# Attention and a token-and-channel mixer on one core: when ScalarE splits the next q and k, and in which order two mixing groups take their chunks

## The chip, the cores and the metric

The kernel runs on one core of a Trainium2 chip. The metric is device microseconds of one execution, the median of several runs. A profile is one further execution with the hardware profiler on; its own time stands beside the runs, because the sum of a prediction is made against the profiled execution.

## The reference, cut to what matters

Eight batches (B), eight heads (H), 576 positions (S), 64 columns a head (D), so 512 channels. Attention sees only the last 128 positions:

```python
scores = (q @ k.T) / sqrt(64) - slope[h] * |i - j|
scores = where(0 <= i - j < 128, scores, -1e9)
attn = softmax(scores)
x = concat_heads(attn @ v)                     # per batch 576 x 512
theta = x @ w_theta
zr, zi = x * cos(theta), x * sin(theta)
y = w_tok_r @ zr + w_tok_i @ zi                # mixes the 576 tokens
u = x + y
out = u + max(u @ w_ch, 0)
```

All products need more precision than one half-width pass gives, so the kernel splits an operand into a high and a low part and multiplies three times (high by high, high by low, low by high).

## The kernel before, in words

Attention works on **pairs** of heads, four pairs a batch. For a pair, `split_pair` (L330) turns the raw q and k (`qr`, `kr`, loaded by `load_pair`, L235) into the parts `qh`, `ql`, `kh`, `kl`: `qh` (L336) and `kh` (L339) are made by ScalarE (ACT), `ql` (L337) by VectorE (DVE), `kl` (L340) by GpSimd (POOL) behind `ql`. `qr` and `kr` are single buffers, so the next pair's load starts once these four have read them. `Pair.scores` multiplies the parts on TensorE (PE); `weigh` adds the bias and finds the row minimum on DVE (L427), and ACT takes the exponential (L430) in place. In the next slot `Pair.flip` turns four 128x128 blocks of the weights into a PSUM bank `t_ps` (L90); ACT copies the bank as the high half of `pt` (L442), DVE makes the low half (L443). There are two `t_ps` banks and four flips a pair. `Head.values` multiplies `pt` by the values (`acc`), and `finish` divides into `x_sb` (L478 to L481, DVE).

After the four pairs of a batch, `turn` goes over five blocks of tokens: it turns `x_sb` into columns (`x_hi`, `x_lo`), multiplies by `w_theta`, takes sine and cosine on ACT (L541 to L547), and writes the products as nine chunks of 128 rows, `z_hi` (ACT, L494 and L556) and `z_lo` (DVE or POOL, L495 and L557). Block 0 gives chunk 8, block 1 chunks 0 and 4, block 2 chunks 1 and 5, block 3 chunks 2 and 6, block 4 chunks 3 and 7.

`mix` (L589) multiplies the chunks by the token weights: eight groups g (half of the tokens by 128 channels), each with a PSUM bank of `ps_m` (three banks, shared with theta, `channels` and the first score tile) and nine chunks, three matmuls to a chunk, in the order 8, 0, 4, 1, 5, 2, 6, 3, 7. Each chunk is one step of a generator. `channels` multiplies the result by `w_ch` and adds it to the output.

**Order of work.** `attend` (L663) computes batch b's attention and at the same time takes steps of batch b-1's mixing. A slot is one pair: flips 0 and 2, `steps[0]` steps of mixing, the next pair's scores (tiles 0, 1, 2), `steps[1]` steps, flips 1 and 3, `steps[2]` steps, the first head's values, scores (tiles 3, 4), then `prepare(p + DEPTH + 2)`, which splits pair p+2 and loads pair p+3, `steps[3]` steps and the second head's values. From batch 2 on the steps of a batch's first slot are 7, 7, 6, 3; of batch 1's first slot 3, 11, 6, 3. I call the first slot of a batch, where the turn's chunks meet the mixing, the **join**.

PE's order is the order in which the code is traced (`keep_in_program_order`). The order on ACT, DVE and POOL is set by the scheduler at compile time, from its own estimates; `tc.issue_after(ins)` binds each instruction traced inside it to stand behind `ins`, but only those on the engine of `ins`. `prepare` stands inside `issue_after(done.ins)`, and `done` is on DVE (L481): `ql` is bound by it, `qh` and `kh` on ACT are not. Each engine works its queue in order, so an instruction that waits holds up all behind it.

Of the kernel before, what the change touches and what calls it, by code (L numbers as in the profile page):

```python
# [17 lines left out]
AF = mybir.ActivationFunctionType  # L18
# [8 lines left out]
PEXP = 14.0  # L27
# [3 lines left out]
DEPTH = 1  # L31
# [19 lines left out]
def attn_moe_kernel(ctx: ExitStack, tc: tile.TileContext, qt, kt, vx, wth, wtok, wch, band, out):  # L51
    nc = tc.nc
# [21 lines left out]
    def mm(*args, **kw):  # L74
        ins = nc.tensor.matmul(*args, **kw)  # L75
        if pinned:
            tc.keep_in_program_order(ins)

    def behind_all(some):
        stack = ExitStack()  # L80
        for ins in some:
            stack.enter_context(tc.issue_after(ins.ins))
        return stack
# [5 lines left out]
    def flipped(*args):  # L89
        ins = nc.tensor.transpose(*args)  # L90
        if pinned:
            tc.keep_in_program_order(ins)
# [142 lines left out]
    def load_pair(p):  # L235
        b, h = divmod(2 * p, H)
        q, kr = (qr_too, kr_too) if p == 1 else (qr, ld.tile([128, S], F32, name="kr"))
        nc.sync.dma_start(out=q[:64, :S], in_=qt[b, h])
        nc.sync.dma_start(out=q[64:, :512], in_=qt[b, h + 1, :, :512])
        nc.sync.dma_start(out=q[64:, S:], in_=qt[b, h + 1, :, 512:])  # L240
        nc.sync.dma_start(out=kr, in_=kt[b, h:h + 2].rearrange("h d s -> (h d) s"))
        return q, kr
# [39 lines left out]
    z_scale, copied = {}, []  # L282
# [95 lines left out]
    class Pair:  # L378
# [53 lines left out]
        def flip(self, bank):  # L432
            t_ps = ps_t.tile([128, 512], F32, name="t_ps")
            for n, (i, e, j) in enumerate(BANKS[bank]):
                flipped(t_ps[:, 128 * n:128 * n + 128], self.sc[i, e][:, 128 * j:128 * j + 128], ident)
            if self.early:
                pt = ptp.tile([128, 512], F32, name="pt")
                nc.scalar.copy(pt, t_ps)
                parts_of = [pt]
            else:  # L440
                pt = ptp.tile([128, 2, 512], F16, name="pt")
                copied.append(nc.scalar.activation(pt[:, 0], t_ps, AF.Copy, scale=2.0 ** PEXP))  # L442
                nc.vector.scalar_tensor_tensor(out=pt[:, 1], in0=t_ps, scalar=2.0 ** PEXP, in1=pt[:, 0],  # L443
                                               op0=ALU.mult, op1=ALU.subtract)
                parts_of = [pt[:, a] for a in range(2)]
            for n, (i, e, j) in enumerate(BANKS[bank]):
                for to in ((0, 1) if i == 0 else (e,)):
                    at = 128 * n + (64 * to if i == 0 else 0)
                    self.pt[i, to, j] = [t[:, at:at + 128] for t in parts_of]
# [139 lines left out]
    def mix(st):  # L589

        xtf, z_hi, z_lo = st["xtf"], st["z_hi"], st["z_lo"]
        u_hi = big.tile([128, 4, S], F32R, name="u_hi")
        u_lo = big.tile([128, 4, S], F32R, name="u_lo")
        st.update(u_hi=u_hi, u_lo=u_lo)
        banks = {}
        seq = (8, 0, 4, 1, 5, 2, 6, 3, 7)

        def part(g, ks):
            hf, m = divmod(g, 4)
            cs = slice(hf * HALF, hf * HALF + HALF)  # L600
            if g not in banks:
                banks[g] = ps_m.tile([128, 512], F32, name="mm")
            y_ps = banks[g]
            for k in ks:
                c = seq[k]
                for n, (z, w) in enumerate(((z_hi, wtk_hi), (z_hi, wtk_lo), (z_lo, wtk_hi))):
                    mm(y_ps[:, :HALF], z[:, c, m * 128:m * 128 + 128], w[:, c, cs],
                       start=(k == 0 and n == 0), stop=(k == 8 and n == 2))
                if k < 8:
                    yield  # L610
            if ks[-1] == 8:
                nc.vector.scalar_tensor_tensor(out=xtf[:, m, cs], in0=y_ps[:, :HALF], scalar=st["back"],  # L612
                                               in1=xtf[:, m, cs], op0=ALU.mult, op1=ALU.add)
                nc.scalar.copy(u_hi[:, m, cs], xtf[:, m, cs])  # L614
                def low(m=m, cs=cs):
                    return nc.gpsimd.tensor_tensor(out=u_lo[:, m, cs], in0=xtf[:, m, cs],  # L616
                                                   in1=u_hi[:, m, cs].bitcast(F32), op=ALU.subtract)

                if st["b"] + 1 < B:
                    lows.append(low)  # L620
                else:
                    low()
                yield

        begun = 2 if st["b"] + 1 < B else 3
        for ks in (range(7), range(7, 9)):
            for g in range(begun):
                yield from part(g, ks)
        for g in range(begun, 8):
            yield from part(g, range(9))  # L630
# [21 lines left out]
    def prepare(p):  # L652

        if 0 <= p - 1 < pairs and p - 1 not in parts:
            parts[p - 1] = split_pair(p - 1, raw.pop(p - 1))
        if p < pairs and p not in raw:
            raw[p] = load_pair(p)
# [5 lines left out]
    def attend(b, x_sb, mixing, chans, first, behind, lowered):  # L663

        for g in range(H // 2):
            p = b * H // 2 + g
            pair = first.pop(0)
            one, two = pair.heads
            new = None
            if p + DEPTH < pairs:  # L670
                new = Pair(p + DEPTH)
                first.append(new)
            measured = []
            if p % 2 and p + 3 < pairs:
                measured.append(((p + 1) // 2 + 1, slice(0, 2)))
            elif p % 2 == 0 and p + 2 < pairs:
                if p == H // 2:
                    measured.append((p // 2 + 1, slice(0, 2)))
                measured.append((p // 2 + 1, slice(2, 4)))
            scaled = p // 2 + 1 if p % 2 and p + 1 < pairs else None  # L680

            def scores(tiles):
                if new is not None:
                    with tc.issue_after(lowered.ins) if b == 1 and g == 0 else nullcontext():
                        new.scores(tiles, behind)

            steps = STEPS[min(g, 2)] if b > 1 else FIRST[g]
            with behind_all((behind, lowered)) if b == 1 and g == 0 else nullcontext():
                pair.flip(0)
                pair.flip(2)  # L690
            step(mixing, steps[0])
            scores(SCORES[0])
            scores(SCORES[1])
            if measured and not (b == 1 and g == 0):
                with tc.issue_after(new.weighed.ins):
                    for some in measured:
                        measure(*some)
            step(mixing, steps[1])
            pair.flip(1)
            pair.flip(3)  # L700
            step(mixing, steps[2])
            if scaled:
                with tc.high_priority(FINISH):
                    spread_first(scaled)
            one.values()
            with tc.high_priority(FINISH):
                done = one.finish(x_sb)
            scores(SCORES[2])
            if scaled:
                with tc.high_priority(FINISH):  # L710
                    spread_scales(scaled)
            with tc.issue_after(done.ins):
                if b == 1 and g == 0:
                    for some in measured:
                        measure(*some)
                if new is not None:
                    new.heads[0].ready()
                prepare(p + DEPTH + 2)
                if b == 1 and g == 0:
                    with behind_all(new.exps):  # L720
                        step(late)
            step(mixing, steps[3])
            if g >= 2 and (b > 1 or g == 3):
                step(chans)
            two.values()
            with tc.high_priority(FINISH):
                done = two.finish(x_sb)
            if new is not None:
                with tc.issue_after(done.ins):
                    done = new.heads[1].ready()  # L730
                    for low in lows:
                        after(low(), done)
                    if b == 1 and g < 3:
                        with behind_all(new.exps):
                            step(late)
            else:
                for low in lows:
                    low()
            lows.clear()
# [156 lines left out]
```

## Time and profile before

| | |
|---|---|
| median of 3 runs (lowest to highest) | 707.63 us (706.1 to 710.97) |
| the profiled execution, its own time | 709.53 us |
| its span, first to last instruction | 707.8 us |
| PE busy | 666.3 us, 94% |
| DVE, ACT, POOL busy | 76%, 71%, 20% |
| mean granted TensorE clock | 0.971 |

The 1.7 us between span and time lie around the span. A matmul record is longer than the distance to the next matmul, because matmuls overlap, so PE's share is not its use at peak. [...]

### The profile page before, as it was taken

Reading aid. Unit: us, or ns where it says so; the run is one execution under the profiler, and the core shown is the slowest. Engines: PE = TensorE matmul, PEld = TensorE weight load, DVE = VectorE, ACT = ScalarE, POOL = GpSimd, SP = SyncE. Lnnn points to the kernel's source line nnn. Section 1 sums busy time; section 2 is a strip of 40 time slices with the busy share of each in tenths; the row PEclk is TensorE's granted clock in tenths of the full one; section 3 lists DMA queues with packets and bytes.
Section 4 is the critical chain, followed back from the end, with each engine's and each line's share of the span. In section 5 each row is a group of like instructions: output and inputs, shape, how many; then the busy total and the mean of one; then the engine's idle time right before and its main releaser. Section 6 shows DMA issues by size and latency. Waiting matters only on the chain.

```text
span 707.8 us, 15986 instructions
## 1 busy us (share of the span) xinstructions
PE 666.3 (94%) x6202; PEld 574.2 (81%) x6202; DVE 540.1 (76%) x1521; ACT 503.0 (71%) x1011; POOL 143.3 (20%) x199
## 2 busy tenths in 40 slices
PE   3779889899999999999999999999999999999998
PEld 2668667789888988888888888789888988889787
DVE  5997698996888769875888768786889768865722
ACT  6998687877957597757966697666976687645810
POOL 3010001440223121221212211211212211310220
PEclk9965998999999999999999999999999999999999
DMA  9943101531023201222022300322021210100001
GB/s 287 309 158 101 39 1 37 159 89 61 26 73 84 91 26 32 84 81 68 26 73 68 105 28 10 106 81 69 26 72 46 82 35 9 36 11 34 26 16 53
DMA packets 32620, 49.86 MB, mean 70 GB/s; under 512 B 5664, under 2 KB 22048, under 8 KB 32544
## 3 DMA queue, kind: packets, MB, share of 16 engines
q1 hardware_dynamic: 32544, 48.84, 22.6%
q8 instruction: 49, 0.80, 0.5%
q14 instruction: 27, 0.22, 0.1%
HBM read 39.39 MB, written 9.44 MB: 69 GB/s over the span
## 4 chain that ended last, share of the span: by engine, by line
PE 42%; ACT 24%; DVE 23%; DMA 6%; issue 2%; SPq 2%; POOL 0%; ACTq 0%; DVEq 0%; POOLq 0%
PE mm L75 30%; PE acc L75 4%; DMA kr<-in_kt_dram 4%; PE t_ps L90 4%; DVE pt L443 4%; ACT s_sb L430 4%; PE s_ps L75 3%; ACT g L546 3%; ACT z_hi L494 2%; ACT g L545 2%; DMA qr<-in_qt_dram 2%; DVE ql L337 2%; DVE g L550 2%; DVE s_sb L427 2%; DVE z_lo L495 2%
## 5 line engine op out<-in xcount | busy, mean ns | idle before, releaser
L75 PE MATMUL mm<-wtk_hi,z_lo 128*128 128x288 f16 x576 | 165.9, 288 | 3.1 <-DVE z_lo L495 3.0
L75 PE MATMUL mm<-wtk_hi,z_hi 128*128 128x288 f16 x576 | 166.2, 289 | 0.6 <-ACT z_hi L494 0.5
L75 PE MATMUL mm<-wtk_lo,z_hi 128*128 128x288 f16 x576 | 165.8, 288 | 0.0
L430 ACT ACTIVATE s_sb<-s_sb,fixed 128x256 f32<-128x256 f32 (+1 forms) x256 | 103.9, 474 | 56.7 <-DVE fixed L427 56.6
L75 PEld LDWEIGHTS <-z_hi 128*128 128x128 f16 x1152 | 109.4, 99 | 31.1 <-ACT z_hi L494 1.5
L443 DVE SCALAR_TENSOR_TENSOR pt<-t_ps,pt 128x512 f16<-128x512 f32 x116 | 76.4, 684 | 35.9 <-ACT pt L442 35.1
L427 DVE CUSTOM_DVE_ANT_0 s_sb<-s_ps,bands 128x256 f32<-128x256 f32 (+1 forms) x256 | 85.5, 384 | 0.3 <-PE s_ps L75 0.3
L75 PEld LDWEIGHTS <-z_lo 128*128 128x128 f16 x576 | 56.6, 98 | 20.8 <-DVE z_lo L495 6.5
L90 PE MATMUL t_ps<-fixed,s_sb 128*128 128x128 f32 x448 | 66.4, 287 | 1.7 <-DVE pt L443 1.7
L616 POOL TENSOR_TENSOR u_lo<-xtf,u_hi 128x288 fp32r<-128x288 f32 x64 | 50.0, 799 | 84.9 <-DVE vl L363 47.6
L442 ACT ACTIVATE pt<-t_ps 128x512 f16<-128x512 f32 x116 | 63.3, 580 | 5.1 <-PE t_ps L90 5.1
L75 PE MATMUL acc<-vh,pt 128*128 128x65 f16 x1044 | 59.7, 194 | 6.4 <-DVE pt L443 4.6
L340 POOL TENSOR_TENSOR kl<-kr,kh 128x576 fp32r<-128x576 f32 x31 | 45.4, 1464 | 99.2 <-DVE ql L337 52.7
L75 PEld LDWEIGHTS <-pt 128*128 128x128 f16 x1566 | 55.2, 98 | 11.0 <-DVE pt L443 6.0
L90 PEld LDWEIGHTS t_ps<-fixed,s_sb 128*128 128x128 f32 x448 | 54.8, 150 | 4.7 <-PE t_ps L90 1.6
L614 ACT CAST u_hi<-xtf 128x288 fp32r<-128x288 f32 x64 | 27.2, 425 | 43.3 <-DVE xtf L612 43.3
L362 POOL MEMSET vh<- 128x5 f16 x58 | 7.0, 121 | 243.2 <-PE acc L75 240.5
L75 PE MATMUL acc<-vl,pt 128*128 128x64 f16 x522 | 55.4, 193 | 0.0
L75 PE MATMUL mm<-wth_hi,x_hi 128*128 128x512 f32 x160 | 47.4, 418 | 1.5 <-DVE x_hi L512 1.5
L75 PE MATMUL mm<-u_hi,wch_hi 128*128 128x288 f32 x256 | 47.2, 306 | 0.0
L612 DVE SCALAR_TENSOR_TENSOR xtf<-mm,fixed,xtf 128x288 f32<-128x288 f32 x64 | 32.0, 509 | 18.7 <-PE mm L75 18.6
L75 PE MATMUL s_ps<-kh,qh 64*128 64x256 f32 (+1 forms) x256 | 44.8, 347 | 0.1
(158 smaller groups left out, 1514.9 us busy)
## 6 DMA issues: line engine op xcount, KB each, us to landing
vb<-in_vx_dram SPq DMA_DIRECT2D x16, 650.0 KB, 5.1
out_dram<-xtf SPq DMA_DIRECT2D x64, 144.0 KB, 1.8
kr<-in_kt_dram SPq DMA_DIRECT2D x31, 288.0 KB, 3.3
qr<-in_qt_dram SPq DMA_DIRECT2D x31, 144.0 KB, 2.8
qr<-in_qt_dram SPq DMA_DIRECT2D x31, 128.0 KB, 2.8
xtf<-in_wch_dram SPq DMA_DIRECT2D x4, 512.0 KB, 4.7
z_hi<-in_wtok_dram SPq DMA_DIRECT2D x2, 576.0 KB, 6.3
z_lo<-in_wtok_dram SPq DMA_DIRECT2D x2, 576.0 KB, 6.3
```

The lines of the kernel that those rows point to most:

```text
L75: ins = nc.tensor.matmul(*args, **kw)
L90: ins = nc.tensor.transpose(*args)
L337: low = nc.vector.scalar_tensor_tensor(out=ql, in0=qr, scalar=sc, in1=qh.bitcast(F32), op0=ALU.mult, op1=ALU.subtract)
L340: rest = nc.gpsimd.tensor_tensor(out=kl, in0=kr, in1=kh.bitcast(F32), op=ALU.subtract)
L427: self.weighed = nc.vector.tensor_tensor_reduce(out=sb, in0=ps, in1=bias, scale=2.0 ** -(2 * self.p % H + 1), scalar=3.0e38, op0=ALU.add, ...
L430: self.exps.append(nc.scalar.activation(sb, sb, AF.Exp, bias=least, scale=-1.0))
L442: copied.append(nc.scalar.activation(pt[:, 0], t_ps, AF.Copy, scale=2.0 ** PEXP))
L443: nc.vector.scalar_tensor_tensor(out=pt[:, 1], in0=t_ps, scalar=2.0 ** PEXP, in1=pt[:, 0], op0=ALU.mult, op1=ALU.subtract)
L546: nc.scalar.activation(g[:n], g[:n], AF.Sin, bias=halfpi[:n], scale=-RAD)
L612: nc.vector.scalar_tensor_tensor(out=xtf[:, m, cs], in0=y_ps[:, :HALF], scalar=st["back"], in1=xtf[:, m, cs], op0=ALU.mult, op1=ALU.add)
L614: nc.scalar.copy(u_hi[:, m, cs], xtf[:, m, cs])
L616: return nc.gpsimd.tensor_tensor(out=u_lo[:, m, cs], in0=xtf[:, m, cs], in1=u_hi[:, m, cs].bitcast(F32), op=ALU.subtract)
```

## The change

Two edits. `Pair.flip` remembers its copy (ACT, L442) as `self.copied`, and `prepare` now also stands behind `pair.copied`, the copy of the slot's last flip (flip 3), which binds `qh` and `kh` on ACT. And the first groups of `mix` take their chunks as five, two, two by turns, where they took seven, two.

```diff
             if self.early:
-                nc.scalar.copy(pt, t_ps)
+                self.copied = nc.scalar.copy(pt, t_ps)
...
-                copied.append(nc.scalar.activation(pt[:, 0], t_ps, AF.Copy, scale=2.0 ** PEXP))
+                self.copied = nc.scalar.activation(pt[:, 0], t_ps, AF.Copy, scale=2.0 ** PEXP)
+                copied.append(self.copied)
...
         begun = 2 if st["b"] + 1 < B else 3
-        for ks in (range(7), range(7, 9)):
+        for ks in (range(5), range(5, 7), range(7, 9)):
             for g in range(begun):
                 yield from part(g, ks)
...
-                prepare(p + DEPTH + 2)
+                with tc.issue_after(pair.copied.ins):
+                    prepare(p + DEPTH + 2)
```

In the changed file the lines from L443 on are one higher, and those from L718 on two.

ACT before, the last slot of a batch from the end of the slot before it, to the start of the turn (`pt` are the copies of flips 0 and 2, then of 1 and 3; `last` and `s_sb` the exponentials; L511 the turn's first copy):

```order
L361 ACTIVATE vh<-vb,fixed 128x5x64
L336 ACTIVATE qh<-qr 128x640
L442 ACTIVATE pt<-t_ps 128x512 x2
L339 CAST kh<-kr 128x576
L430 ACTIVATE last_104<-last_104,fixed 128x192
...
L442 ACTIVATE pt<-t_ps 128x512 x2
L614 CAST u_hi<-xtf 128x288
...
L336 ACTIVATE qh<-qr 128x640
L361 ACTIVATE vh<-vb,fixed 128x5x64
L339 CAST kh<-kr 128x576
L511 CAST x_hi<-t_ps 128x4x64
```

The same stretch of ACT in the change:

```order
L361 ACTIVATE vh<-vb,fixed 128x5x64
L442 ACTIVATE pt<-t_ps 128x512 x2
L430 ACTIVATE last_104<-last_104,fixed 128x192
...
L442 ACTIVATE pt<-t_ps 128x512 x2
L615 CAST u_hi<-xtf 128x288
L336 ACTIVATE qh<-qr 128x640
L339 CAST kh<-kr 128x576
...
L361 ACTIVATE vh<-vb,fixed 128x5x64
L512 CAST x_hi<-t_ps 128x4x64
```

`qh` and `kh` stood ahead of, between or behind the slot's first copies, one slot ahead of their `ql`, and once ahead of the turn's first copy; now they stand behind the copies of flips 1 and 3, in the slot of their `ql`. The order on SP, which issues the loads, is unchanged.

PE before, at a join from batch 2 on (matmuls of chunks; `mm_3662` is group 0's bank, `mm_3714` group 1's, `mm_3684` the first score tile, `t_ps_3736` flip 1):

```order
L75 MATMUL mm_3662<-wtk_hi_121,z_hi_3373 128x288
...
L75 MATMUL mm_3662<-wtk_hi_121,z_lo_3374 128x288
L75 MATMUL mm_3684<-kh_3297,qh_3295 128x192
...
L75 MATMUL mm_3714<-wtk_hi_121,z_hi_3373 128x288
...
L75 MATMUL mm_3714<-wtk_hi_121,z_lo_3374 128x288
L90 MATMUL t_ps_3736<-fixed_103,s_sb512_3264 128x128 x4
```

PE in the change, the same stretch (`mm_3678` is group 1's bank, `mm_3685` the first score tile):

```order
L75 MATMUL mm_3662<-wtk_hi_121,z_lo_3374 128x288
...
L75 MATMUL mm_3678<-wtk_hi_121,z_hi_3373 128x288
...
L75 MATMUL mm_3678<-wtk_hi_121,z_lo_3374 128x288
L75 MATMUL mm_3685<-kh_3297,qh_3295 128x192
...
L75 MATMUL mm_3678<-wtk_hi_121,z_hi_3373 128x288
...
L75 MATMUL mm_3662<-wtk_hi_121,z_hi_3373 128x288
...
L75 MATMUL mm_3678<-wtk_hi_121,z_lo_3374 128x288
L90 MATMUL t_ps_3736<-fixed_103,s_sb512_3264 128x128 x4
```

Ahead of the scores stood seven chunks of group 0; now five of group 0 and two of group 1. Behind them stood seven of group 1; now three of group 1, then chunks 2 and 6 for each group. Chunks 3 and 7 come behind the flips in both.

DVE before, at the same join (`z_lo` from `g` and `f` of block 4 are chunks 3 and 7):

```order
L443 SCALAR_TENSOR_TENSOR pt<-t_ps,pt 128x512
L550 SCALAR_TENSOR_TENSOR g<-x_sb,fixed,g 128x512
L427 ISA last_105,fixed<-mm,bands 128x192
...
L495 TENSOR_TENSOR z_lo<-g,z_hi 128x512
L427 ISA s_sb_3692,fixed<-s_ps,bands 128x128
...
L260 TENSOR_REDUCE peak_108<-vb 128x2
L495 TENSOR_TENSOR z_lo<-f,z_hi 128x512
```

DVE in the change:

```order
L444 SCALAR_TENSOR_TENSOR pt<-t_ps,pt 128x512
L427 ISA last_105,fixed<-mm,bands 128x192
...
L551 SCALAR_TENSOR_TENSOR g<-x_sb,fixed,g 128x512
...
L260 TENSOR_REDUCE peak_108<-vb 128x2
L496 TENSOR_TENSOR z_lo<-g,z_hi 128x512
L496 TENSOR_TENSOR z_lo<-f,z_hi 128x512
```

The weighing of the scores moved ahead of chunk 3's `z_lo`; the same instructions stand ahead of chunk 7's.

## Rows read from the trace of the kernel before

**Rows 1.** Windows view: us, busy of each engine, clock, DMA, GB/s; a whole batch.
```profile
255.00:330.00 75.00, 73.13 (x750) 63.48 (x749) 60.22 (x179) 53.27 (x111) 17.37 (x24) 1.00 0.23 66
```

**Rows 2.** Waits of PE (us in total, times, longest), 160 to 640 us.
```profile
PE acc L75 <- DVE pt L443: 2.6, 6, 0.5
PE mm L75 <- DVE z_lo L495: 2.1, 5, 0.4
PE mm L75 <- DVE x_hi L512: 0.7, 1, 0.7
PE acc L75 <- ACT pt L442: 0.6, 1, 0.6
PE t_ps L90 <- DVE pt L443: 0.6, 1, 0.6
```

**Rows 3.** Waits of PE's weight loads, 160 to 640 us.
```profile
PEld L75 <- DVE z_lo L495: 3.6, 5, 0.7
PEld L75 <- DVE pt L443: 3.6, 7, 0.6
PEld mm L75 <- DVE x_hi L512: 1.4, 3, 0.9
...
PEld L75 <- ACT pt L442: 0.9, 2, 0.7
```

**Rows 4.** Waits of ACT, 97 to 708 us.
```profile
ACT s_sb L430 <- DVE fixed L427: 55.3, 26, 3.6
...
ACT qh L336 <- DMA qr<-in_qt_dram: 14.3, 19, 2.1
ACT kh L339 <- DMA kr<-in_kt_dram: 12.1, 16, 2.4
```

**Rows 5.** Timeline of ACT (start us, us, what, [idle before]), a batch's last slot.
```profile
306.74 0.74 ACT L336 ACTIVATE qh<-qr 128x640 fp32r<-128x640 f32 x1 [0.59 <-DMA qr<-in_qt_dram]
307.39 1.06 ACT L442 ACTIVATE pt<-t_ps 128x512 f16<-128x512 f32 x2
310.86 0.67 ACT L339 CAST kh<-kr 128x576 fp32r<-128x576 f32 x1 [2.41 <-DMA kr<-in_kt_dram]
...
313.18 1.05 ACT L442 ACTIVATE pt<-t_ps 128x512 f16<-128x512 f32 x2
...
317.51 1.71 ACT L430 ACTIVATE s_sb<-s_sb,fixed 128x256 f32<-128x256 f32 x4 [2.96 <-DVE fixed L427]
```

**Rows 6.** Timeline of DVE, the same slot.
```profile
313.78 1.29 DVE L443 SCALAR_TENSOR_TENSOR pt<-t_ps,pt 128x512 f16<-128x512 f32 x2 [1.96 <-ACT pt L442]
...
316.32 0.81 DVE L337 SCALAR_TENSOR_TENSOR ql<-qr,qh 128x640 fp32r<-128x640 f32 x1
```

**Rows 7.** Timeline of all engines at a join: chunk 6, chunk 7, chunk 3.
```profile
268.41 0.10 PEld L75 LDWEIGHTS <-z_lo 128*128 128x128 f16 x1 [0.73 <-DVE z_lo L495]
...
272.92 0.68 DVE L495 TENSOR_TENSOR z_lo<-f,z_hi 128x512 f16<-128x512 f32 x1
...
273.29 0.29 PE L75 MATMUL mm<-wtk_hi,z_hi 128*128 128x288 f16 x1
...
273.41 0.29 PE L75 MATMUL mm<-wtk_lo,z_hi 128*128 128x288 f16 x1
```

**Rows 8.** Waits of PE, 97 to 160 us.
```profile
PE acc L75 <- DVE pt L443: 1.9, 2, 1.0
```

**Rows 9.** Waits of PE's weight loads, 97 to 160 us.
```profile
PEld L75 <- DVE z_lo L495: 1.7, 3, 0.9
```

**Rows 10.** Windows: batch 1's join, then its first slots.
```profile
103.00:109.60 6.60, 5.57 (x23) 2.44 (x21) 6.47 (x19) 6.57 (x12) 0.00 (x0) 0.50 0.00 0
118.00:147.00 29.00, 27.03 (x318) 22.91 (x318) 28.83 (x96) 23.47 (x51) 12.25 (x15) 1.00 0.44 129
```

**Rows 11.** Waits of PE, 640 to 708 us.
```profile
PE mm L75 <- DVE z_lo L495: 0.5, 1, 0.5
```

**Rows 12.** Waits of PE's weight loads, 640 to 708 us.
```profile
PEld L75 <- DVE z_lo L495: 1.2, 2, 0.8
```

## The prediction, made before the changed kernel ran

> **What bounds the kernel now.** I read the windows first: in one whole batch PE is busy 73.1 of 75 us, DVE 60.2, ACT 53.3 [rows 1]. So PE sets the pace, and an edit is worth what it takes out of PE's waits; ACT and DVE time counts only where PE stands behind it. Next come the waits, of PE and of its weight loads side by side [rows 2, 3]. The first are too short, because a matmul record lasts 0.29 us though the next one starts 0.12 us later [rows 7], so that part of a stop is hidden under the last record; the second are too long, since loads run ahead. The truth lies between. From 160 to 640 us PE stops for the low half of pt (2.6 to 3.6 us), for its high half (0.6 to 0.9), for a flip's bank that DVE has not read out (0.6), for the turn's first columns (0.7 to 1.4) and for z_lo (2.1 to 3.6). Third, who is late: ACT waits 14.3 us for the loads of qr and 12.1 us for kr [rows 4], in its queue, with other work behind.
>
> **Moving q and k on ACT (batches 2 to 7).** Nothing is added: the casts still take 0.74 and 0.67 us [rows 5], in another place. In a batch's last slot qh waited 0.59 us for its load and ran ahead of the first pt copies, and kh stood 2.41 us ahead of the exponentials, so the second pt copies came at 313.18 [rows 5]. DVE sat idle 1.96 us for them and made the low halves from 313.78 [rows 6], and PE waited for these. Without casts and waits the first copies can come 0.59 + 0.74 = 1.3 us earlier, and the exponentials by at least the 2.41 + 0.67 = 3.1 us that kh held them, if DVE has weighed the scores by then. The stops that are some 0.6 us long cannot survive that. Where the casts now stand, behind the second copies, ACT was idle before the next four exponentials (2.96 us here, 55.3 us in all [rows 5, 4]), and the two casts take 1.41 us of it. Behind them in ACT's queue stand a cast of u_hi, the exponentials, and vh; DVE's ql waits for qh, but starts only at 316.32 [rows 6], some 2 us after qh would end (copies to 314.2, one u_hi, then qh). The load has landed: kr's late one ended ACT's wait at 310.86 [rows 5]. SP's order is the same, and loads still start behind ql and kl, so qr and kr have most of a slot to land instead of being asked for on landing.
>
> I take the stops for pt at the upper bound, 3.6 + 0.9 = **4.5 us**, because they are many and short, where the matmul's record hides most; the bank's stop at **0.6 us**. The turn's first column copy stood behind qh, vh and kh with their waits, and now stands behind vh alone: **1.2 us**, near the upper bound of 1.4, as two of the three stops appear in the weight loads only. Together 6.3 us; bounds 4.5 (PE's rows, all of them) to 6.5, and zero if DVE is late by itself.
>
> **Five, two, two.** At five joins PE reaches chunk 6 before its z_lo is written (0.73 us in the load's row, 0.4 in PE's [rows 7, 2]). In the new order chunks 2 and 6 come behind the scores, and this stop goes. But what is late next is chunk 7. Its z_lo starts on DVE at 272.92 and lasts 0.68, so it ends at 273.60 [rows 7], with no idle time before it in its row, and the same DVE instructions stand ahead of it as before, so it does not come earlier. PE began chunk 3 at 273.29 and reads chunk 7's z_lo as the sixth matmul, 5 x 0.12 later, at 273.9. Started 0.6 us earlier it would read at 273.3, and must wait for 273.6, while chunk 3's z_lo has also moved back on DVE behind the weighing. So of 0.6 us a join I credit only 0.15, over five joins **0.7 us**; bounds 0 and the 3.6 us of rows 3. Where no attention follows, in the last batch, three groups now take fifteen chunks before block 3 is needed, and the stop goes: 0.5 to 1.2 us [rows 11, 12], I take **0.9**.
>
> **Batch 1.** [...] Eleven steps behind the scores are 33 matmuls; at half clock 0.24 us each, 7.9 us, so with seven chunks ready PE is busy throughout and part of the stops goes. I take 1.2. In the slots behind, PE waits 1.9 us for pt [rows 8], but DVE is busy 28.8 of 29 us there [rows 10]: DVE is the bound, and an earlier copy on ACT gives little. I take 0.8 of the 1.9. Together **2.0 us**; bounds 0 and 1.7 + 1.9 = 3.6.
>
> **Sum.** 6.3 + 0.7 + 0.9 + 2.0 = 9.9 us. Against the profiled execution's own 709.53 (span 707.8 and 1.7 around it) that gives 699.6; the median of the runs, 707.63, lies 1.9 lower and would give 697.7. I take **698.5**, between them.
>
> **Rivals.**
> *DVE takes over.* The stops for pt are put down to DVE, which also weighs, splits and divides. For it: DVE is full in batch 1 [rows 10], and at the joins it has no gap. Against: in later slots it idles for ACT (1.96 us in rows 6). If only half of the 6.3 us goes, nothing at the five joins, and 0.9 + 1.0 elsewhere, the gain is 5.1 us: 703.5 by the same middle. Chance 0.25.
>
> *TensorE's clock comes back sooner at batch 1's join.* The granted clock stood at 0.50 for the whole stretch in which PE kept stopping [rows 10]. With the stops gone, the same 33 matmuls at full clock take 4.0 us instead of 7.9. ACT's and DVE's work allows about 2 us of that, and if at the five joins the weighing delays chunk 7 less than I think (another 2 us), the gain is 13.9 us: 694.7. Chance 0.13. [...]
>
> *The casts wait for loads in their new place: slower.* They now stand ahead of the four exponentials and of ql, so a load that lands behind the second pt copies holds ACT, then DVE's ql and the weighing behind it. It decides where a load lands later than ACT's idle time covers, 2.96 - 1.41 = 1.5 us behind the copies [rows 5]. For it: kr's wait of 2.41 shows that loads can be late. Against: each load now has most of a slot. If one slot in each of seven batches waits 2.4 us uncovered and the gain for pt goes too, it is 7 x 2.4 - (9.9 - 6.3) = 13 us slower, 722 by the same middle. Chance 0.05.
>
> That the change does nothing is excluded: the three queues are in another order.
>
> **Chances and range.** The forecast has 0.57, its own range 694 to 703. About 1% (7.1 us) is what a measurement here can tell from no change, so faster means under 700.5. Of the forecast three quarters lie there, of the clock rival all, of DVE's hardly any: 0.57 x 0.75 + 0.13 + 0.01 = 0.57. Slower 0.05, the rest, 0.38, within 1%. The range for 8 in 10 reaches from 691 (all upper bounds, 6.5 + 3.6 + 1.2 + 3.6, and the clock's 2, are 16.9 under the median) to 705, which takes in DVE's rival.
>
> **What would show it.** Right: no wait of qh or kh for a DMA in ACT's waits; the stops for pt, and for the turn's first columns, gone from PE's; at the joins no stop at the sixth chunk, and a new, shorter one at chunk 3's or 7's z_lo behind the flips. Wrong: PE's waits for pt as long as before with DVE busy ahead of them (then DVE was the cause); joins shorter by 0.5 us each (then chunk 7 was not the limit); batch 1's 118 to 147 us much shorter (then ACT held DVE there); waits of qh for its load behind the second copies.

## The result and the profile after

| | before | changed |
|---|---|---|
| median of 13 runs each (lowest to highest) | 709.67 us (705.76 to 712.51) | 702.25 us (699.19 to 705.42) |
| ratio, 95% interval | | 0.9897 [0.9871, 0.9923] |
| profiled execution, own time and span | 709.53, 707.8 us | 699.19, 697.4 us |

The change is faster by 1.0%, 7.4 us by the medians (5.5 to 9.2 by the interval) and 10.3 us between the two profiled executions. The forecast was 698.5 us, its sum 699.6 for the profiled execution.

To see where the time went I cut every trace at the same four matmuls: the first transpose of each turn, the first scores and the first values of batch 1. For the changed kernel these rows of PE's timeline are the cuts (start us, us, what):

```profile
99.63 0.36 PE L75 MATMUL mm<-kh,qh 128*128 128x192 f32 x1 [1.50 <-DVE f L543]
...
113.49 0.19 PE L75 MATMUL acc<-vh,pt 128*128 128x65 f16 x1
...
161.41 0.38 PE L90 MATMUL t_ps<-fixed,x_sb 128*128 128x128 f32 x2
...
631.49 0.38 PE L90 MATMUL t_ps<-fixed,x_sb 128*128 128x128 f32 x2
```

The table has the distances between the cuts, from the traces of all kernels of this study ("join" is from the first scores of batch 1 to its first values, "slots" from there to batch 1's turn, "six batches" from there to the last turn, "end" the rest):

| kernel | start to batch 0's turn | turn to scores | join | slots | six batches | end |
|---|---|---|---|---|---|---|
| before | 76.32 | 24.99 | 12.77 | 47.08 | 479.76 | 66.83 |
| changed | 75.56 | 24.07 | 13.87 | 47.92 | 470.08 | 65.93 |
| changed, a second profile | 80.69 | 23.51 | 12.19 | 49.03 | 470.03 | 65.91 |
| casts alone | 75.22 | 25.85 | 12.88 | 47.89 | 471.20 | 66.83 |
| five, two, two alone | 81.07 | 25.08 | 12.20 | 47.06 | 480.42 | 65.91 |
| two load buffers | 81.72 | 24.89 | 14.48 | 46.68 | 471.21 | 66.82 |
| old place, two buffers | 82.34 | 22.73 | 13.05 | 47.75 | 478.16 | 66.82 |
| old place but for first slots | 82.48 | 25.72 | 14.72 | 47.78 | 471.28 | 66.82 |
| z_lo on POOL | 81.54 | 23.81 | 14.72 | 47.80 | 470.14 | 65.92 |
| unpacking spread | 75.91 | 24.07 | 13.86 | 51.73 | 473.00 | 65.92 |
| peak later | 76.91 | 25.52 | 12.19 | 49.08 | 469.82 | 65.92 |
| batch 1 as before | 80.56 | 23.54 | 12.19 | 47.06 | 470.07 | 65.91 |
| pt first | 81.70 | 24.93 | 10.74 | 49.56 | 470.10 | 65.92 |
| casts later, pt first | 80.78 | 23.54 | 10.74 | 47.74 | 470.04 | 65.92 |

In the kernels whose casts wait for no load, the last two columns repeat to 0.1 us wherever the code is the same and the granted clock stays at full; two profiles have a stretch at half clock in the six batches ("five, two, two alone" and "unpacking spread", below), and the kernel before was profiled once only. The first four columns do not repeat (second row against third), and whoever compares single profiles must leave them out. So the change takes 9.7 us out of the six batches and 0.9 out of the end; up to batch 1's turn it gives nothing (161.16 us before, 161.41 after). By distances between turns, batch 2 takes 79.79 us in both kernels; batches 3 to 6 took 79.5 to 81.5 us each before and take 78.59 each, and batch 7 took 77.12 and takes 75.93.

The waits say the same. Waits of PE and of its loads, 160 to 640 us, have one row left, against [rows 2, 3]:

```profile
PEld L75 <- DVE z_lo L496: 3.2, 10, 0.4
```

From 640 us on there is none, against [rows 11, 12]. ACT's longest waits, 97 to 708 us, have no load among them any more, against [rows 4]:

```profile
ACT s_sb L430 <- DVE fixed L427: 56.2, 38, 3.1
ACT u_hi L615 <- DVE xtf L613: 28.7, 12, 4.5
ACT last L430 <- DVE fixed L427: 19.1, 18, 1.6
ACT x_hi L512 <- PE t_ps L90: 12.4, 7, 3.5
...
```

ACT's last slot of a batch, against [rows 5] (timeline, with the idle time before):

```profile
305.30 1.07 ACT L442 ACTIVATE pt<-t_ps 128x512 f16<-128x512 f32 x2
...
309.97 1.09 ACT L442 ACTIVATE pt<-t_ps 128x512 f16<-128x512 f32 x2 [0.18 <-PE t_ps L90]
...
311.26 0.75 ACT L336 ACTIVATE qh<-qr 128x640 fp32r<-128x640 f32 x1
311.90 0.67 ACT L339 CAST kh<-kr 128x576 fp32r<-128x576 f32 x1
315.62 1.71 ACT L430 ACTIVATE s_sb<-s_sb,fixed 128x256 f32<-128x256 f32 x4 [3.06 <-DVE fixed L427]
```

The second copies now come 4.7 us behind the first (5.8 before) and wait for PE's flips, not PE for them. Both casts run without a wait for their loads, and ACT is still idle for 3.06 us ahead of the exponentials.

In one whole batch PE is busy 74.94 of 75 us, against 73.13 in [rows 1]:

```profile
255.00:330.00 75.00, 74.94 (x764) 65.43 (x763) 60.54 (x179) 55.72 (x114) 17.47 (x24) 1.00 0.23 67
```

### The profile page after: what moved, and what is told of

Same layout as the page of the kernel before. It is cut to its first block, busy times and chain, and to the rows that moved or that the text cites. A ratio compares the mean times of both kernels' runs of the same rounds, so it can differ in the third digit from the quotient of the medians.

```text
span 697.4 us, 15987 instructions
## 1 busy us (share of the span) xinstructions
PE 662.0 (95%) x6202; PEld 573.2 (82%) x6202; DVE 542.0 (78%) x1521; ACT 502.9 (72%) x1011; POOL 143.3 (21%) x199
## 4 chain that ended last, share of the span: by engine, by line
PE 61%; DVE 21%; ACT 14%; DMA 2%; issue 1%; SPq 0%; POOL 0%; DVEq 0%; ACTq 0%; POOLq 0%
PE mm L75 42%; PE t_ps L90 7%; PE acc L75 6%; PE s_ps L75 6%; DVE s_sb L427 3%; DVE z_lo L496 2%; DVE pt L444 2%; ACT g L547 2%; ACT g L546 2%; ACT z_hi L495 2%; DVE g L551 2%; DMA qr<-in_qt_dram 2%; DVE peak L260 1%; DVE f L551 1%; DVE f L543 1%
## 5 line engine op out<-in xcount | busy, mean ns | idle before, releaser
L427 DVE CUSTOM_DVE_ANT_0 s_sb<-s_ps,bands 128x256 f32<-128x256 f32 (+1 forms) x256 | 85.2, 384 | 1.5 <-PE s_ps L75 1.5
L442 ACT ACTIVATE pt<-t_ps 128x512 f16<-128x512 f32 x116 | 63.1, 582 | 5.8 <-PE t_ps L90 5.8
L75 PE MATMUL acc<-vh,pt 128*128 128x65 f16 x1044 | 57.8, 194 | 3.0 <-DVE pt L444 2.0
L645 DVE SCALAR_TENSOR_TENSOR xtf<-mm,xtf 128x288 f32<-128x288 f32 x64 | 29.0, 454 | 22.1 <-PE mm L75 20.9
```

Of the source, the lines that this page charges most:

```text
L427: self.weighed = nc.vector.tensor_tensor_reduce(out=sb, in0=ps, in1=bias, scale=2.0 ** -(2 * self.p % H + 1), scalar=3.0e38, op0=ALU.add, ...
L442: self.copied = nc.scalar.activation(pt[:, 0], t_ps, AF.Copy, scale=2.0 ** PEXP)
L645: nc.vector.scalar_tensor_tensor(out=xtf[:, e, cs], in0=o_ps[:, :HALF], scalar=0.0, in1=xtf[:, e, cs], op0=ALU.max, op1=ALU.add)
```

## The experiments

Besides the cuts I use PE's **stops**: the distance from one matmul's start to the next, less the median distance of that pair of forms in the same trace, where it is over 0.1 us. From 160 us on they fell by 10.2 us in all: from 5.5 to 0 before the values (which wait for pt), 1.4 to 0 at the turns' first columns, 1.0 to 0 at the flips, 0.4 less at other places, 3.8 to 1.8 at z_lo. In batch 1, 97 to 160 us, they rose by some 2 us; there a matmul at half clock (0.24 us behind the one before it, where full clock has 0.12) counts as a stop too.

### Each edit alone

```diff
-        for ks in (range(5), range(5, 7), range(7, 9)):
+        for ks in (range(7), range(7, 9)):
```

> The casts of q and k behind the slot's last copies, the mixing groups still by seven and two. The stops that PE lost between the two profiles are 5.5 us for pt, 1.4 at the turn's first columns, 1.0 for a flip's bank and 2.0 for z_lo. If each edit has its own stops, this one takes 5.5 + 1.4 + 1.0 = 7.9 us off, 1.1% (ratio 0.989), and PE still stops 0.6 us at the sixth chunk of five joins. Rival: the stops for pt go because both edits together change the order of the joins; then this kernel gains 4 us or less (ratio 0.994 or more).

Measured: 704.98 us, ratio 0.9892 [0.9855, 0.9928]. Six batches in 471.20 us, 8.6 less than before, and a batch every 78.8 us; nothing is gained at the end. PE's waits from 165 to 650 us keep the one row that the other edit is about, as long as in [rows 2]:

```profile
PE mm L75 <- DVE z_lo L496: 2.2, 5, 0.4
```

The first theory holds, with 8.6 us for the 7.9 expected. The other edit alone is the kernel before with

```diff
-        for ks in (range(7), range(7, 9)):
+        for ks in (range(5), range(5, 7), range(7, 9)):
```

> Five, two, two alone, the casts where they were. If each edit has its own stops: 2.0 us faster (ratio 0.997), a stop of 0.2 us a join in place of 0.6 us, and the stops for pt stay at 4 to 6 us. Rival: what a join gains is lost again at the next stop for pt, since DVE and ACT have the same work in the same order; then no change (ratio 1.000), with longer stops for pt in the first slots.

Measured: 710.54 us, ratio 0.9992 [0.9967, 1.0018]. The end has its 0.9 us, but the six batches take 480.42, 0.7 more than before. Its waits of PE, 165 to 650 us:

```profile
PE acc L75 <- DVE pt L443: 2.3, 5, 0.5
PE t_ps L90 <- DVE pt L443: 1.5, 2, 0.9
PE acc L75 <- ACT pt L442: 0.9, 2, 0.6
PE mm L75 <- DVE x_hi L512: 0.5, 1, 0.5
```

The wait for z_lo is gone from PE's rows, and the waits for pt and the flips' bank are 4.7 us where [rows 2] had 3.8: some of what the joins give, the next late copies take. But this profile has something that the kernel before has not: the granted clock fell in batch 6, behind two stops for pt of 0.65 and 0.49 us (window, then matmuls inside it, 0.24 us apart where full clock has 0.12):

```profile
536.50:539.90 3.40, 3.40 (x23) 2.33 (x23) 3.29 (x15) 1.69 (x5) 1.41 (x1) 0.50 0.19 46
...
536.99 0.45 PE L75 MATMUL mm<-wtk_hi,z_lo 128*128 128x288 f16 x1
537.23 0.45 PE L75 MATMUL mm<-wtk_hi,z_hi 128*128 128x288 f16 x1
```

By the starts of matmuls this stretch costs PE 1.6 us. Without it the six batches would take some 478.8 us (an estimate from these two numbers), 1.0 less than before. With the casts moved, the same edit is worth 471.20 - 470.08 = 1.1 us in the six batches (0.22 a batch) and 0.9 at the end. So the 480.42 does not show that the second edit pays only behind the first. The runs do not decide it either: the first theory's ratio of 0.997 and the rival's 1.000 both lie in the interval. Whether the two edits add up stays open.

### Was it the waits for the loads, or the place in the queue?

```diff
-    ld = ctx.enter_context(tc.tile_pool(name="ld", bufs=1))
+    ld = ctx.enter_context(tc.tile_pool(name="ld", bufs=2))
...
-    qr = const.tile([128, S + 64], F32, name="qr")
+    qrs = [const.tile([128, S + 64], F32, name=f"qr{k}") for k in range(2)]
```

> The kernel before with two buffers for the raw q and two for the raw k, nothing else: a load no longer waits until the slot's low parts are made, and is asked for a slot ahead. The scheduler by itself then puts both casts behind the second copies, as the change does by a binding. If late loads were the cause (as an order of the queue and as waits), this gains the same as the casts alone, 7 to 8 us (ratio 0.989), with no wait of ACT for qr or kr. Rival: the earlier loads collide with the values' loads or make other work late; then under 4 us.

Measured: 707.46 us, ratio 0.9941 [0.992, 0.9962]. Six batches in 471.21 us, the same as the casts alone; no wait of ACT for `qr` or `kr`. The median gains less; in the traces of all three kernels with two buffers batch 0, which is ordered in another way there, ended late (81.7 to 82.5 us), but whether that is the reason no run parts from the scatter of that column. Since the scheduler here moves the casts too, place and wait still go together. The next kernel parts them:

```diff
+            ahead = b > 1 and p + DEPTH + 1 < pairs
+            if ahead:
+                with tc.issue_after((pair.exps[-1] if g else behind).ins):
+                    q_cast = cast_q(p + DEPTH + 1, raw[p + DEPTH + 1])
...
+                with tc.issue_after(q_cast.ins) if ahead else nullcontext():
+                    pair.flip(0)
+                    pair.flip(2)
+            if ahead:
+                with tc.issue_after(pair.copied.ins):
+                    k_cast = cast_k(p + DEPTH + 1)
```

> From batch 2 on, two buffers for the raw loads, and the casts bound to their old place: q's ahead of the slot's first copies, k's ahead of the exponentials; groups by seven and two. It parts the two things that the change took away. If the waits for the loads made the stops (14.3 and 12.1 us of waiting on ACT), the casts' own 0.74 + 0.67 us ahead of the copies are covered, and this is within 1.5 us of the casts alone (ratio about 0.990). If the place made them, the stops for pt stay at 3 us or more and the gain is under 4.5 us (ratio 0.994 or more).

Measured: 714.66 us, ratio 1.005 [1.0025, 1.0075], and 478.16 us for the six batches. By the total the place would be to blame. The waits of PE, 160 us to the end, say otherwise:

```profile
PE t_ps L90 <- DVE pt L455: 7.5, 5, 1.5
PE t_ps L90 <- DVE peak L295: 0.5, 1, 0.5
PE mm L75 <- DVE z_lo L507: 0.5, 1, 0.5
```

No stop for pt before the values is left; there is one new stop of 1.66 us by starts (1.5 in the row) in each of five first slots, where I had put the casts ahead of copies that are late anyway. The kernel before has no such stop, so it tells of my edit and not of the old place. So once more, with the first slots as in the change:

```diff
-            ahead = b > 1 and p + DEPTH + 1 < pairs
+            ahead = b > 1 and g > 0 and p + DEPTH + 1 < pairs
```

> As the kernel with the casts at their old place and two buffers, but in the first slot of each batch the casts stand where the change puts them, so that the 1.66 us that PE stopped there for a flip's bank goes away. If the waits for the loads were what made the stops for pt, none of those stops comes back, and from the first turn to the end this takes 6 to 8 us less than the kernel before (631.4 us there), as the casts alone do. If the place alone costs, PE stops 3 us or more for pt in the later slots and gains under 4 us there.

Measured: 709.99 us, ratio 0.9972 [0.9951, 0.9994] (with the late batch 0 again), and 471.28 us for the six batches: the same as the casts alone, with PE's waits 165 to 650 us in one row.

```profile
PE mm L75 <- DVE z_lo L507: 2.2, 5, 0.5
```

It was the waits. One of them in the kernel before: the first exponential's tile was weighed at 309.55 us, and ACT took it at 311.44, behind the kh that had waited for its load until 310.86 [rows 5] (timelines of DVE and ACT):

```profile
309.20 0.35 DVE L427 CUSTOM_DVE_ANT_0 last<-mm,bands 128x192 f32<-128x192 f32 x1
...
311.44 0.45 ACT L430 ACTIVATE last<-last,fixed 128x192 f32<-128x192 f32 x1
```

In the later slots of a batch the casts' 1.4 us ahead of the copies cost nothing, if the loads have landed; in the first slot they cost 1.66 us.

### What is left at the joins

```diff
-                with tc.issue_after(new.weighed.ins):
+                with tc.issue_after(new.weighed.ins), tc.issue_after((new.weighed if g else lowered).ins):
                     for some in measured:
```

> The changed kernel, with DVE's peak (0.81 us) behind the last two z_lo at the five joins instead of ahead of them. If DVE's chain to the seventh chunk's z_lo sets the 0.225 us stop that is left, the stop goes and each batch takes 0.2 us less (78.6 to 78.4), 1.1 us in all. Rival: the two low halves of pt that wait behind the peak now come later and PE stops for them; then no gain.

Measured: 702.21 us, ratio 0.9883 [0.9844, 0.9923]; six batches in 469.82 us, 0.26 less than the change. The 0.225 us stop at chunk 7 is gone, and PE's loads wait for pt instead, 165 to 650 us:

```profile
PEld L75 <- DVE pt L444: 1.4, 5, 0.3
```

DVE's chain did set chunk 7, and the rival holds for most of the 1.1 us: behind that chain PE now stops for the low halves of pt, 0.3 us at a time.

### Batch 1

```diff
-                    split_z(c, z, nc.gpsimd if st["b"] and i < 3 else nc.vector)
+                    split_z(c, z, nc.gpsimd if i < 3 else nc.vector)
```

> The changed kernel, with four of the eight low halves of z in batch 0's turn (0.68 us each on DVE) made on POOL, as in the later batches. DVE has 2.7 us less to do at batch 1's join, so the flips' bank comes free earlier and the stop of 2.4 us shrinks by 1 us or more. If DVE's work from 118 to 147 us is the bound of batch 1, the rows behind it move as a whole and batch 1 ends 1 to 2.7 us earlier, turn to turn (85.9 us there). Rival: batch 1 is held by ACT or by the loads; then the lead is lost again by 141 us and the turn comes at the same distance. POOL's z_lo is slower, so PE may stop for z at chunks 1 and 5: then no gain or up to 1 us lost.

Measured: 703.89 us, ratio 0.9899 [0.9842, 0.9957]; the join took 14.72 us, the slots 47.80. The 14.72 cannot be set beside the change's 13.87: here the clock was at 0.50 from 105.7 to 109.1 and from 115.9 to 119.3 us, in the change only in the one stretch shown below. But the stop that the edit was to shorten, PE's for the flips' bank, did not shrink (2.8 us by starts, 2.4 in the change). With 2.7 us less to do, DVE waits for ACT's sines instead (waits of DVE, 100 to 120 us):

```profile
DVE g L551 <- ACT g L547: 1.7, 2, 1.5
DVE f L543 <- ACT f L542: 1.7, 1, 1.7
DVE pt L444 <- ACT pt L442: 1.3, 1, 1.3
...
```

So the waits speak against DVE alone holding the join. For the slots behind:

```diff
-                if b == 1 and g == 0:
-                    with behind_all(new.exps):
-                        step(late)
...
-            if g >= 2 and (b > 1 or g == 3):
+            if g >= 2 and b > 1:
...
-                    if b == 1 and g < 3:
+                    if b == 1:
```

> The changed kernel, with the four chunks of the channel weights unpacked one a slot in batch 1 (two stood in the first slot), and the channels of batch 0 begun a slot later. It takes 0.86 + 0.68 us of DVE's work out of each of the slots from 118 to 147 us and puts one chunk behind 147, where DVE has room. If DVE is the bound there, batch 1 ends 1 to 1.6 us earlier, turn to turn. Rival: ACT holds DVE there; then the same turn-to-turn time within 0.3 us.

Measured: 707.13 us, ratio 0.9971 [0.9944, 0.9998], slower than the change. The last chunk of weights came too late for the channels (waits of PE, 99 to 167 us, beside the 3.2 us for pt that the change also has):

```profile
PE mm L75 <- ACT wch_hi L198: 4.9, 1, 4.9
PE t_ps L90 <- DVE pt L444: 3.2, 3, 2.3
...
```

Behind PE's stop for it, 5.0 us by starts, the clock fell (0.50 from 161.5 to 168 us), which is why the six batches have 473.00. The question itself got half an answer: from the second slot's first scores to the fourth's PE took 27.2 us, and 27.7 in the changed kernel. DVE is busy for 26.47 us of that stretch here and for 27.47 in the changed kernel, so half of the 1.0 us that DVE has less to do comes back.

Next, the change without batch 1, and the change with DVE's order turned at batch 1's join:

```diff
-                with tc.issue_after(pair.copied.ins):
+                with tc.issue_after(pair.copied.ins) if b > 1 else nullcontext():
...
-        for ks in (range(5), range(5, 7), range(7, 9)):
+        for ks in ((range(5), range(5, 7), range(7, 9)) if st["b"] else (range(7), range(7, 9))):
```

> The change for batches 2 to 7 alone: in batch 1 the casts and the mixing groups are as in the kernel before. If batch 1 gained nothing, this is as fast as the full change, and the time from batch 1's turn to the next (84.8 us before, 85.9 after) is at 84.8 to 85.9. My forecast had batch 1 at 2.0 us of gain: then this kernel would be 2.0 us slower there than the full change. If instead batch 1 loses by the change, the turn comes 1.0 us earlier than with it. From batch 1's turn to the end: 536.0 us by every theory, as with the full change.

Measured: 701.14 us, ratio 0.9867 [0.9809, 0.9925]. Slots 47.06 us, as before and as with five, two, two alone; five kernels with the casts bound there and the clock full have 47.75 to 47.92 (changed, casts alone, both of the old place, z_lo on POOL). So binding the casts costs batch 1 0.8 us. And the join takes 12.19 us with seven and two (here, with the clock at 0.50 from 105.1 to 108.4 us), 12.20 with five, two, two (alone, with the clock at 1.00): neither the new groups nor the clock in that stretch brought the join time. From batch 0's turn to its next this kernel takes 82.80 us and the kernel before 84.84, with the same code in batch 1, so a difference of 2 us there between two single profiles shows nothing.

```diff
-                    with tc.issue_after(lowered.ins) if b == 1 and g == 0 else nullcontext():
+                    with tc.issue_after(pair.low.ins) if b == 1 and g == 0 else nullcontext():
                         new.scores(tiles, behind)
```

(`pair.low` is DVE's instruction for the low half of the last flip's pt.)

> The changed kernel, with the first pair's low halves of pt (2 x 0.6 us on DVE) ahead of the weighing of the new scores (1.4 us) at batch 1's join alone. PE's stop of 2.4 us for the flip's bank at 108.6 us shrinks to about 1.0 us. If it was that stop behind which the granted clock fell to half for the next 13 matmuls (110 to 113 us), the clock stays at full there, and the first values of batch 1 come 1.4 + 1.6 = 3.0 us earlier behind the join. If the slots behind are held by DVE anyway, all of it but 0 to 0.5 us is lost again by the next turn; if not, the turn comes up to 3.0 us earlier (85.9 us turn to turn with the change, 82.9 then). Rival: the clock falls all the same, and 1.4 us or less is gained.

Measured: 701.42 us, ratio 0.9865 [0.9798, 0.9933]. PE's stop at the flips is 0.94 us instead of 2.4, and the join 10.74 us, 1.45 under 12.19, as expected; but the slots take 49.56, and turn to turn it is 85.2 us. What is gained at the join is lost behind it, partly to the clock, which fell in the second slot here (0.61 from 133 to 137 us).

### The version that the runs point to, beside the change

Both edits of the last two kernels that paid: casts bound from batch 2 on, pt first at batch 1's join, five, two, two everywhere.

> A version out of what the runs showed: the change, with the casts bound only from batch 2 on, and at batch 1's join DVE makes the first pair's low halves of pt ahead of the new scores' weighing. From the first values of batch 1 to its turn the kernels with the casts in their old place took 47.0 to 47.1 us, those with them bound mostly 47.8 or 47.9; from the join to those values it took 12.2 us without a fall of the clock and 10.8 with pt first. If these add up, turn to turn in batch 1 is about 2.2 us under the changed kernel at the same clock in batch 0's turn (85.9 us), and the rest is the same 536.0 us; ratio to the kernel before about 0.986. Rival: the slots behind give the join's 1.4 us back, as with pt first alone (49.5 us from values to turn); then it is no faster than the change.

> The changed kernel again, beside the version above on the same chip, so that the two can be compared: ratio to the kernel before 0.990 as in its first runs, 536.0 us from batch 1's turn to the end, and a batch every 78.6 us.

Measured on one chip: 700.7 us for the new version, ratio 0.9855 [0.9828, 0.9883]; 702.52 us for the change, 0.9882 [0.9849, 0.9915]. Turn to turn in batch 1 takes 82.0 us, against 84.7 and 85.9 in the two profiles of the change; the join has its 10.74 us, the slots give 0.7 of that back (47.74 against 47.06). The runs alone do not part the two, as the intervals overlap; by the traces the new version is 2.7 and 3.9 us shorter than the change from batch 0's turn on (618.0 against 620.7 and 621.9), of which up to 2 us can be scatter, as the same code differed by that much there.

## Why the prediction was right, and where not

**Moving q and k on ACT**, forecast 6.3 us: right in mechanism, mis-sized. It took 8.6 us out of the six batches, all from batch 3 on, more than my upper bound of 6.5. I had taken the waits' rows [rows 2, 3] for bounds. They are none: by starts of matmuls the stops for pt were 5.5 us, not at most 4.5; the bank 1.0, not 0.6; the columns 1.4, not 1.2; and 0.4 us stood at places that the waits do not list. That the casts are free in their new place held, with the same idle time of ACT behind them. My "some 2 us" between qh's end and ql does not follow from the numbers beside it (314.2 + 0.74 leaves at most 1.4), but 2.4 us were measured (qh ends at 312.0, ql starts at 314.4). That the loads' waits were the cause is shown by the two-buffer kernels; the place mattered only in the first slots.

**Five, two, two**, forecast 0.7 at five joins and 0.9 in the last batch: measured 1.1 and 0.9. The new stop came where I put it. The join in the changed kernel, against [rows 7] (chunk 7's z_lo on DVE; the matmuls of chunk 3 with z_lo, and of chunk 7):

```profile
272.93 0.68 DVE L496 TENSOR_TENSOR z_lo<-f,z_hi 128x512 f16<-128x512 f32 x1
...
273.06 0.30 PE L75 MATMUL mm<-wtk_hi,z_lo 128*128 128x288 f16 x1
...
273.66 0.10 PEld L75 LDWEIGHTS <-z_lo 128*128 128x128 f16 x1 [0.36 <-DVE z_lo L496]
273.66 0.30 PE L75 MATMUL mm<-wtk_hi,z_lo 128*128 128x288 f16 x1
```

I had PE there at 273.3 and held until 273.6; it could have read at 273.43 and was held until 273.66. Whether this gain at the joins needs the casts moved is open, as the edit alone did not settle it.

**Batch 1**, forecast 2.0 us: this step failed, in both halves. The join's 1.2 us, of the 1.7 us for z_lo in [rows 9]: what I expected happened and brought no time. From 103 to 109.6 us the granted clock was 1.00 instead of the 0.50 of [rows 10], at which the matmuls of a chunk started 0.24 us apart, and PE had its eleven steps done at 106.1 us; then it stood until DVE had made the first pair's pt, and behind that stop the clock fell (windows of the changed kernel: us, busy of PE, loads, DVE, ACT, POOL, clock):

```profile
103.00:109.60 6.60, 3.64 (x27) 2.30 (x25) 6.01 (x18) 6.57 (x14) 0.00 (x0) 1.00 0.00 0
109.60:113.20 3.60, 3.60 (x18) 2.33 (x17) 2.29 (x4) 2.47 (x6) 0.00 (x0) 0.53 0.00 0
118.00:147.00 29.00, 26.27 (x312) 22.19 (x311) 28.82 (x95) 22.63 (x50) 12.11 (x14) 1.00 0.44 128
```

The wait itself, and a second one that is new in batch 1 (timeline of PE):

```profile
108.56 0.41 PE L90 MATMUL t_ps<-fixed,s_sb 128*128 128x128 f32 x2 [2.25 <-DVE pt L444]
...
129.01 0.39 PE L75 MATMUL mm<-fixed 128*128 128x4 f32 x2 [0.67 <-DVE fixed L272]
```

I had asked only whether PE would have matmuls for the eleven steps, not who frees the bank of the next flips: ahead of that pt DVE weighs the new scores for 1.4 us. The slots' 0.8 us had the wrong sign: there the binding costs 0.8 us. Of that the second wait explains most, 0.73 us by starts: DVE's order behind the moved copies put the small L272 beside a POOL instruction (below). That stop stands in all nine traces with the casts bound in batch 1 and in none of the five others.

**Rivals.** DVE did not take over in the later batches; it did what that rival says only in batch 1. The clock rival's condition came true, its time did not: the clock was at full where it had been at half, and the next stop ate it. That it was at full because stops had gone is not shown. In the kernel before, the clock had fallen by 103.0 us, ahead of the join's stops for z (the first at 104.3 us, by starts) and behind a stop of 1.50 us before the first scores, which the changed kernel has as well. "Old place, two buffers", with seven and two, kept full clock through batch 1, and the version that the runs point to, with five, two, two, did not (windows of the kernel before, of old place, and of that version):

```profile
99.00:102.80 3.80, 2.30 (x23) 1.64 (x21) 3.03 (x6) 2.61 (x5) 0.00 (x0) 1.00 0.02 4
...
97.00:166.00 69.00, 61.72 (x665) 51.13 (x664) 65.31 (x184) 55.80 (x114) 16.92 (x22) 1.00 0.28 79
...
105.40:108.60 3.20, 3.20 (x17) 2.09 (x17) 2.75 (x5) 3.20 (x7) 0.00 (x0) 0.50 0.00 0
```

These traces do not decide what made the difference. The rival's second half, joins that gain more, was there in small, 1.1 for 0.7 us. The casts never waited for loads in their new place.

**The sum** came within 0.4 us of the profiled execution (699.6 against 699.19) by luck: 2.7 us too little for batches 2 to 7 met 3.0 too much for batch 1 (2.0 forecast, 1.0 lost from turn to turn in this profile), and the start was 0.8 us earlier. Against the median of 702.25 us the forecast of 698.5 is 3.75 us low: the kernel before itself has a median of 709.67 over 13 runs where three had given 707.63, and the change was profiled in one of its early starts.

## What to carry to other kernels

An instruction that waits for a load belongs behind the work that others wait for, or its load belongs a buffer earlier; both cured the same 8.6 us, and the cast's own time cost next to nothing outside the first slots. Size stops by the distance between the starts of matmuls, not by the rows of waits, which here fell short even as an upper bound. When a stop goes, walk on to the next instruction that takes a buffer (a flip's bank here), and price an edit together with the stop behind it. Read the granted clock of both traces before comparing a stage of them: one stretch at half clock, worth 1.6 us, is more than five, two, two gives in the six batches.

## What the runs showed of the hardware

**The clock fell at another stop in another execution of the same kernel.** In the second profile of the change PE stopped 2.4 us for the same flips and the clock stayed; it fell in the next slot (windows of that profile; one with both 0.50 and 1.00 in it reads between):

```profile
70.00:76.00 6.00, 6.00 (x33) 5.78 (x33) 4.10 (x14) 2.18 (x5) 0.00 (x0) 0.50 0.00 0
109.00:113.00 4.00, 1.27 (x9) 0.60 (x7) 4.00 (x16) 3.97 (x8) 0.00 (x0) 1.00 0.00 0
131.00:136.00 5.00, 4.35 (x46) 3.07 (x43) 4.39 (x16) 2.58 (x6) 2.23 (x2) 0.66 0.45 134
```

Between these two profiles, the one with the fall took 1.7 us more at the join (13.87 against 12.19) and the other 1.1 more in the slots (49.03 against 47.92). In the version with the best batch 1 it fell at 105 to 109 us (0.57), where PE stops 0.60 us for z_lo in the change, and the join still took the 10.74 us of "pt first", which had 1.00 there. In "five, two, two alone" it fell late, behind stops for pt that the kernel before has too (0.63 and 0.49 us at 450 us) without a fall (1.00 from 440 to 460 us). In the two profiles of the change the falls lay some 20 us apart, behind different stops: the first behind the 2.25 us for the flips, the second where PE had been busy for 1.23 of 2.00 us (129 to 131 us, at 1.00). What sets the point of a fall is not shown. The same holds for batch 0: from 70 to 76 us the second profile ran at 0.50 and the first at 1.00 (below), and its turn came 5.1 us later.

```profile
70.00:76.00 6.00, 5.74 (x68) 5.19 (x67) 6.00 (x26) 3.38 (x7) 0.12 (x1) 1.00 0.36 109
```

**A small DVE instruction took four times as long beside a POOL instruction.** L272 takes 0.21 to 0.23 us in 31 of the 32 times in the two profiles before and after. Once, in batch 1 of the change, it took 0.87 us and ended at 128.96 us, with the POOL instruction that had started 0.43 us ahead of it and ended at 128.94 (timeline of both engines):

```profile
128.09 0.87 DVE L272 TENSOR_SCALAR fixed<-fixed 128x4 f32<-128x4 f32 x1
...
127.66 1.28 POOL L199 TENSOR_TENSOR wch_lo<-xtf,wch_hi 128x512 fp32r<-128x512 f32 x1
```

The second profile of the change has it too, 0.86 us. In the first it was 0.65 us longer than elsewhere, and PE waited 0.67 us for it. The other traces agree: in all nine with the casts bound in batch 1, L272 starts some 0.4 us into this POOL instruction and takes 0.86 to 0.87 us, and in the five others it starts at 1.0 us or later and takes 0.22 us, once 0.37. Why the two end together is not shown. "Batch 1 as before" is one of the five:

```profile
129.69 1.28 POOL L199 TENSOR_TENSOR wch_lo<-xtf,wch_hi 128x512 fp32r<-128x512 f32 x1 [2.60 <-ACT wch_hi L198]
130.84 0.22 DVE L272 TENSOR_SCALAR fixed<-fixed 128x4 f32<-128x4 f32 x1
```
